# Linear attention and two gated FFNs on one core: q and x transposed in 32x32 blocks on VectorE, with loads and stores in 128-byte runs

## The chip, the cores and the metric

One core of a Trainium2 chip runs the whole kernel. The metric is the device time of one execution in microseconds (us). The kernel before took 1865.18 us, the median of three runs (1863.83 to 1867.42). Engines go by these names: PE is TensorE (PEld its weight loads), DVE is VectorE, ACT is ScalarE, POOL is GpSimd, SP is SyncE, which here only issues DMAs.

## The reference

8 batches, 8 heads, 576 positions, 64 values a head; all in float32.

```python
kv = np.einsum('bhsd,bhse->bhde', k, v)
out = np.einsum('bhsd,bhde->bhse', q, kv)
rms = np.sqrt(np.mean(out * out, axis=-1, keepdims=True) + 1e-06)
attn_out = out / rms * g_norm                      # g_norm: 64 values, the same for every head
x = attn_out.transpose(0, 2, 1, 3).reshape(4608, 512)
# first FFN (512 -> 1536 -> 512)
x = (1 / (1 + exp(-(x @ w_gate))) * (x @ w_val)) @ w_out
# second FFN, own weights
g = x @ w_gate2
x = (g * (1 / (1 + exp(-g))) * (x @ w_val2)) @ w_out2
```

## The kernel before

**The FFNs.** The 4608 tokens are cut into 9 blocks of 512, and each FFN's 1536 hidden values into 12 slices of 128. Four phases follow each other: slices 0 to 5 of the first FFN over all blocks, slices 6 to 11 of it, and the same for the second. Float32 products are made from a high and a low part, in three passes. Only the first phase shares its time with the attention and touches x in its first layout. In it `gv_plain` (L524) makes gate and value of one slice in 24 matmuls, `out_parts` (L645) multiplies the slice before by w_out in 12. The first block (block 0) is worked on while the weights of the six slices arrive: each weight tile is loaded raw (`raw`, L308 and L311), and VectorE, ScalarE and GpSimd turn it into its two parts (`o1` to `o7`, `hi`, `lo`; `u` and `s` are their buffers). From block 1 on these weights lie ready in SBUF.

**The attention.** It works on 36 tiles of 128 tokens, four to a block. Nine tiles make a pair of batches: four of the first batch, one mixed tile (i = 4) of the last 64 positions of both, four of the second batch. A tile goes through these stages, each one called for a later tile than the one before it (lags 0, 1, 3, 3, 4, 5 tiles):

- `tok_q`: the tile's q is copied out of the batch's q buffer `qm` into `qs` (ScalarE, L130; for batch 0 VectorE, L128). The mixed tile reads `qr`, loaded on its own.
- `tok_a`: four PE transposes of 128x128 into `qTp` (L165), then a ScalarE copy to `qT` (L167).
- `tok_b`: PE multiplies qT by the block-diagonal kv (L181, for the mixed tile L179), ScalarE squares the result.
- `tok_r`: VectorE sums the squares (L188), GpSimd makes the reciprocal root `y`.
- `tok_n`: VectorE multiplies by y into `xn` (L208).
- `tok_c`: four PE transposes into `xTp` (L214), ScalarE multiplies by g while it copies out to `xT` (L216; in this layout the 64 values of g lie along the partitions, in `gcol`), and one DMA stores the tile to `xd` in DRAM (L222), from where the FFN loads it as `xl` (L471).

The first four tiles (block 0) run in a prologue written out by hand (the string `PROLOGUE`); the others by `attention_steps`. The q of a batch lies in the positions p*4 + r of its partition p, so one load brings 1 KB a packet (`load_main`, L100), and the batch's 128-token tile r is every fourth position. Output rows are written in the same pattern.

**What sets the order.** The steps of the attention, the preparation of x and the weights stand in queues (`att`, `xq`, `wq`, `pq`) with due times, and `tick()` between matmuls takes from each what is due. `AHEAD = (16, 20, 24, 28, 32)` says of tiles in which block they are due: tiles before 16 in block 0, before 20 in block 1, and so on. ScalarE and GpSimd run what they are given in program order from the start; VectorE too from block 4 of the first phase on. PE, SP and, until there, VectorE get their order from a scheduler that works with a cost model. SP issues all DMAs in one stream, each when its buffer is free. The tiles named above share nine buffers of one tag (`ta`, `TA = 9`); the q and the k of a batch use two large buffers in turn (`st0`, `st1`); raw weights have three buffers.

Of the kernel before, what the change touches and what calls it, by code (L numbers as in the profile page):

```python
# [10 lines left out]
F32 = mybir.dt.float32  # L11
# [3 lines left out]
ALU = mybir.AluOpType  # L15
# [9 lines left out]
def attention_two_ffn(ctx: ExitStack, tc: tile.TileContext, q, k, v, g_norm, weights, out):  # L25
# [8 lines left out]
    nc = tc.nc  # L34
    B, H, S, D = q.shape
    DM = H * D
    DFF = weights[0][0].shape[1] // 2
    NT = B * S
    P = 128
    NB = 512  # L40
    NBLK = NT // NB
    TPB = NB // P
    KD = DM // P
    NP = H // 2
    R = 4
    SM = R * P
# [6 lines left out]
    dr = ctx.enter_context(tc.tile_pool(name="dr", bufs=1, space=DRAM))  # L53
# [6 lines left out]
    at = at_ctx.enter_context(tc.tile_pool(name="at", bufs=1, side="right"))  # L60
# [15 lines left out]
    mask = at.tile([P, P], F32, name="mask")  # L76
    gcol = at.tile([P, 1], F32, name="gcol")
    mhalf = at.tile([P, H], F32, name="mhalf")
    make_identity(nc, ident)
    nc.vector.memset(mask, 0.0)  # L80
    for e in range(2):
# [2 lines left out]


    MANUAL = (0, 4)
    TA = 9
    kvt, qt, kvps, kvbd, qT, xn, xd = {}, {}, {}, {}, {}, {}, {}
    for j in range(NBLK):
        xd[0, j] = dr.tile([P, KD, NB], F32, name=f"xd{j}")  # L90
        xd[1, j] = dr.tile([P, KD, NB], F32, name=f"yd{j}")

    def load_main(b, src, nm, halves=1):

        rows = src[b, :, :SM, :].rearrange("h (p r) d -> p h r d", r=R)
        slot = "v" if nm == "v" else f"st{b % 2 if b > 1 else 'kq'.index(nm)}"
        t = kvt[b, nm] = at.tile([P, H, R, D], F32, tag=slot, name=f"{nm}m")
        for z in range(halves):
            hs = slice(z * H // halves, (z + 1) * H // halves)
            nc.sync.dma_start(out=t[:, hs], in_=rows[:, hs])  # L100
# [9 lines left out]
        load_main(b, v, "v", 2 if b == 0 else 1)  # L110

    def load_q(b):
        load_main(b, q, "q", 2 if b == 0 else 1)

    def load_qr(bp):
        t = at.tile([P, H, D], F32, tag="qr", name="qr")
# [4 lines left out]
    def run_of(b, nm, r, hs=slice(0, H)):  # L121

        if (b, nm, r) not in kvt:
            tag, n = ("ta", TA) if b == 0 else (nm + "s", 2)
            kvt[b, nm, r] = at.tile([P, H, D], F32, tag=tag, bufs=n, name=f"{nm}s")
        t, src = kvt[b, nm, r][:, hs], kvt[b, nm][:, hs, r, :]
        if b == 0:
            nc.vector.tensor_copy(out=t, in_=src)  # L128
        else:
            nc.scalar.activation(t, src, AF.Copy)  # L130

    def bank_for(early, name):

        if early:
            return ps_o.tile([P, NP, P], F32, tag="o", name=name)
        return ps_g.tile([P, NP, P], F32, tag="g", name=name)
# [13 lines left out]

    def tok_q(tau):
        bp, i = divmod(tau, TP)
        if i != R:
            run_of(2 * bp + (i > R), "q", i if i < R else i - R - 1)

    def tok_a(tau):
        bp, i = divmod(tau, TP)
        ps = ps_g.tile([P, NP, P], F32, tag="g", name="qTp")
        for hp in range(NP):
            hs = slice(2 * hp, 2 * hp + 2)  # L160
            if i == R:
                src = qt[bp][:, hs, :]
            else:
                src = kvt[2 * bp + (i > R), "q", i if i < R else i - R - 1][:, hs, :]
            nc.tensor.transpose(ps[:, hp, :], src, ident)  # L165
        qT[tau] = at.tile([P, NP, P], F32, tag="ta", bufs=TA, name="qT")
        nc.scalar.activation(qT[tau], ps, AF.Copy)  # L167
# [3 lines left out]
    def tok_b(tau):  # L171
# [10 lines left out]
        ost[tau] = ps.rearrange("p a (b d) -> p (a b) d", d=D)  # L182
        sqt[tau] = at.tile([P, H, D], F32, tag="ta", bufs=TA, name="sq")
        nc.scalar.activation(sqt[tau], ost[tau], AF.Square)
# [20 lines left out]
    def tok_n(tau):  # L205
        y = sqt.pop(tau)
        xn[tau] = at.tile([P, H, D], F32, tag="ta", bufs=TA, name="xn")
        nc.vector.tensor_tensor(out=xn[tau], in0=ost.pop(tau), in1=y.unsqueeze(2).to_broadcast([P, H, D]), op=ALU.mult)  # L208

    def tok_c(tau):  # L210
        t = xn.pop(tau).rearrange("p (a b) d -> p a (b d)", b=2)
        ps = bank_for(tau < TPB, "xTp")
        for hp in range(NP):
            nc.tensor.transpose(ps[:, hp, :], t[:, hp, :], ident)  # L214
        x = at.tile([P, NP, P], F32, tag="ta", bufs=TA, name="xT")
        nc.scalar.activation(x, ps, AF.Identity, scale=gcol)  # L216
        j, c = divmod(tau, TPB)
        cs = slice(c * P, (c + 1) * P)
        if j == 0:
            xh, xlo = x_tiles(0, 0)  # L220
            split(xh[:, :, cs], xlo[:, :, cs], x)
        nc.sync.dma_start(out=xd[0, j][:, :, cs], in_=x)  # L222
# [57 lines left out]
    def split(hi, lo, src):  # L280
        nc.scalar.activation(hi, src, AF.Copy)  # L281
        sub(lo, src, hi.bitcast(F32))
# [170 lines left out]
    def x_tiles(ph, j):  # L453
        if (ph, j) not in xt:
            if PH[ph][3]:
                s = "RL"[((ph - 1) * NBLK + j) % 2]
                xt[ph, j] = [late[s].tile([P, 5 - i // 2, 2, HB], F32R, tag=f"x{i}", name=f"x{i}") for i in range(3)]
            else:
                xt[ph, j] = [x0p.tile([P, KD, NB], F32R, tag="x", name=f"x{b}") for b in range(2)]
        return xt[ph, j]  # L460
# [217 lines left out]
    def evac(ph, j, i):  # L678
        f = PH[ph][0]
        ps = ops.pop((ph, j, i))  # L680
        if starts(ph):
            t = wk.tile([P, NB], F32, tag="ye", bufs=4, name="ye")
            nc.scalar.activation(t, ps, AF.Copy)
        else:
            if (ph, j, i) not in part:
                load_part(ph, j, i)
            t = part.pop((ph, j, i))
            add(t, t, ps)
        if not ends(ph):
            if (ph, j) not in pd:  # L690
                pd[ph, j] = dr.tile([P, 4, NB], F32, name=f"pd{ph}_{j}")
            nc.sync.dma_start(out=pd[ph, j][:, i, :], in_=t)
        elif f == 0:
            nc.sync.dma_start(out=xd[1, j][:, i, :], in_=t)
        else:
            bp, n = divmod(j * TPB + i, TP)
            if n == R:
                for e in range(2):
                    r0 = (2 * bp + e) * S + SM
                    nc.sync.dma_start(out=out[r0:r0 + SR, :], in_=t[e * SR:(e + 1) * SR])  # L700
            else:
                r0 = (2 * bp + (n > R)) * S
                r = n if n < R else n - R - 1
                nc.sync.dma_start(out=out[r0:r0 + SM, :].rearrange("(p r) e -> p r e", r=R)[:, r, :], in_=t)

# [73 lines left out]
    for t, z in steps:  # L781
        j = next((j for j, a in enumerate(AHEAD) if t < a), len(AHEAD))
# [3 lines left out]
    wq.run(2)  # L786
    for e in range(2):
        nc.sync.dma_start(out=gcol[e * D:(e + 1) * D], in_=g_norm.unsqueeze(1))
    for z in range(2):
        for r in range(R):  # L790
            run_of(0, "k", r, slice(z * H // 2, (z + 1) * H // 2))
# [106 lines left out]
```

## Time and profile before

| | before |
|---|---|
| median of three runs | 1865.18 us |
| profiled execution | 1871.27 us, span 1869.5 us |
| granted PE clock, mean | 0.993 |
| busy: PE, PEld | 1833.5 us (98%), 1650.1 us (88%) |
| busy: DVE, ACT, POOL | 1152.0 (62%), 686.6 (37%), 597.7 us (32%) |
| DMA queue | 179312 packets, 253.80 MB, 41.6% of 16 engines |

Busy shares are means over stages with different limits, so the rows further down are cut by stretch of time. In a row of busy time by stretch stand the start and end in us from the span's start, the length, and then the busy us (with the count of instructions) of PE, PEld, DVE, ACT and POOL; an engine without work in a row that is filtered by a tile is left out; the last three numbers are the granted clock of TensorE, the mean busy share of the 16 DMA engines, and GB/s. In a short stretch the share can come out a little over 1. In the chain of waits a DMA's length runs from its issue to its landing. The PE rows of a timeline give busy time of pipelined matmuls, whose modelled ends overlap; the starts are the sounder number. In the groups by line, the tile written stands left of the arrow and those read right of it, then partitions x elements and the type.

### The profile page before, as it was taken

Reading aid. Unit: us, or ns where it says so; the run is one execution under the profiler, and the core shown is the slowest. Engines: PE = TensorE matmul, PEld = TensorE weight load, DVE = VectorE, ACT = ScalarE, POOL = GpSimd, SP = SyncE. Lnnn points to the kernel's source line nnn. Section 1 sums busy time; section 2 is a strip of 40 time slices with the busy share of each in tenths; the row PEclk is TensorE's granted clock in tenths of the full one; section 3 lists DMA queues with packets and bytes.
Section 4 is the critical chain, followed back from the end, with each engine's and each line's share of the span. In section 5 each row is a group of like instructions: output and inputs, shape, how many; then the busy total and the mean of one; then the engine's idle time right before and its main releaser. Section 6 shows DMA issues by size and latency. Waiting matters only on the chain.

```text
span 1869.5 us, 29756 instructions
## 1 busy us (share of the span) xinstructions
PE 1833.5 (98%) x11620; PEld 1650.1 (88%) x11620; DVE 1152.0 (62%) x1946; ACT 686.6 (37%) x1318; POOL 597.7 (32%) x600
## 2 busy tenths in 40 slices
PE   5899999999999999999999999999999999999999
PEld 5688888888888899999999999999999999999998
DVE  4784444444334576676666777777775566666664
ACT  3564444443323333333333343334343323232321
POOL 1574233220111433424424334334332222222221
PEclk8899999999999999999999999999999999999999
DMA  7896554336333724424429423233228222222212
GB/s 225 237 276 186 166 155 141 113 119 236 124 107 99 279 91 153 130 91 143 134 96 368 167 97 107 88 111 107 79 97 327 90 69 68 69 68 69 68 52 68
DMA packets 179453, 255.70 MB, mean 137 GB/s; under 512 B 23920, under 2 KB 123760, under 8 KB 177008
## 3 DMA queue, kind: packets, MB, share of 16 engines
q1 hardware_dynamic: 179312, 253.80, 41.6%
q8 instruction: 91, 1.49, 0.3%
q14 instruction: 50, 0.41, 0.1%
HBM read 164.10 MB, written 89.65 MB: 136 GB/s over the span
## 4 chain that ended last, share of the span: by engine, by line
PE 94%; DVE 2%; DMA 2%; POOL 1%; issue 1%; ACT 1%; SPq 0%; DVEq 0%; ACTq 0%
PE gv L586 43%; PE o L659 24%; PE gv L524 15%; PE o L645 8%; PE kvps L145 2%; PE ops L181 1%; DMA vm<-in_v_dram 1%; POOL y L191 1%; PE xTp L214 1%; DMA raw<-in_moe_w_gate_dram 1%; PE qTp L165 1%; DVE a L188 0%; PE ops L179 0%; DVE u L275 0%; POOL a L189 0%
## 5 line engine op out<-in xcount | busy, mean ns | idle before, releaser
L586 PEld LDWEIGHTS gv<-x,wgv 128*128 128x128 f32 x6804 | 821.3, 190 | 8.3 <-PE gv L586 0.6
L586 PE MATMUL gv<-x,wgv 128*128 128x256 f32 x6804 | 823.6, 282 | 0.4 <-DMA wgv<-wd 0.4
L524 PE MATMUL gv<-x,wgv 128*128 128x512 f32 x1296 | 318.9, 395 | 1.3 <-ACT qT L167 1.3
L659 PE MATMUL o<-wo,h 128*128 128x512 f32 x1296 | 311.3, 395 | 0.0
L659 PEld LDWEIGHTS o<-wo,h 128*128 128x128 f32 x1296 | 239.6, 188 | 53.8
L524 PEld LDWEIGHTS gv<-x,wgv 128*128 128x128 f32 x1296 | 238.8, 188 | 50.5 <-POOL u L200 1.7
L574 POOL TENSOR_TENSOR h<-v,h 128x512 fp32r<-128x512 f32 x81 | 112.3, 1386 | 482.3 <-ACT h L570 482.3
L275 DVE TENSOR_TENSOR u<-u,gv 128x512 f32<-128x512 f32 x162 | 110.8, 684 | 217.5 <-PE gv L586 206.7
L496 POOL TENSOR_TENSOR x<-xl,x 128x512 fp32r<-128x512 f32 x108 | 146.0, 1361 | 147.4 <-ACT x L493 131.4
L645 PE MATMUL o<-h,wo 128*128 128x512 f32 x648 | 169.1, 401 | 5.2 <-ACT h L281 5.2
L574 POOL TENSOR_TENSOR h<-w,h 128x512 fp32r<-128x512 f32 x81 | 105.2, 1299 | 207.6 <-ACT h L570 207.6
L659 PE MATMUL o<-h,wo 128*128 128x512 f32 x648 | 156.3, 396 | 2.4 <-POOL h L574 1.7
L645 PEld LDWEIGHTS o<-h,wo 128*128 128x128 f32 x648 | 119.1, 189 | 31.2 <-issue 6.0
L659 PEld LDWEIGHTS o<-h,wo 128*128 128x128 f32 x648 | 120.0, 188 | 29.6 <-POOL h L574 2.3
L557 ACT ACTIVATE w<-v 128x256 f32<-128x256 f32 x81 | 33.9, 418 | 303.3 <-DVE v L275 303.3
L570 ACT ACTIVATE h<-w 128x512 fp32r<-128x512 f32 x81 | 51.2, 633 | 192.2 <-PE o L659 95.3
L493 ACT ACTIVATE x<-xl 128x512 fp32r<-128x512 f32 x189 | 115.1, 623 | 12.0 <-DVE xl L272 9.6
L534 DVE TENSOR_TENSOR sg<-sg,gv 128x512 f32<-128x512 f32 x54 | 37.1, 686 | 106.9 <-PE gv L524 106.9
L557 ACT ACTIVATE v<-g 128x256 f32<-128x256 f32 x81 | 33.9, 418 | 152.5 <-DVE g L275 152.5
L570 ACT ACTIVATE h<-v 128x512 fp32r<-128x512 f32 x81 | 51.2, 632 | 104.9 <-DVE v L563 104.9
L496 DVE TENSOR_TENSOR x<-xl,x 128x512 fp32r<-128x512 f32 x81 | 70.8, 874 | 22.5 <-ACT x L493 22.4
L275 DVE TENSOR_TENSOR g<-u,gv 128x512 f32<-128x512 f32 x81 | 55.6, 686 | 41.3 <-PE gv L586 40.1
(88 smaller groups left out, 1910.1 us busy)
## 6 DMA issues: line engine op xcount, KB each, us to landing
wgv<-wd SPq DMA_DIRECT2D x18, 1792.0 KB, 9.7
pd<-ye SPq DMA_DIRECT2D x72, 256.0 KB, 3.0
pl<-pd SPq DMA_DIRECT2D x72, 256.0 KB, 4.2
xl<-yd SPq DMA_DIRECT2D x72, 256.0 KB, 2.9
xl<-xd SPq DMA_DIRECT2D x68, 256.0 KB, 3.1
wd<-raw SPq DMA_DIRECT2D x54, 256.0 KB, 2.8
raw<-in_moe_w_gate_dram SPq DMA_DIRECT2D x24, 512.0 KB, 4.5
raw<-in_moe_w_val_dram SPq DMA_DIRECT2D x24, 512.0 KB, 4.4
```

Of the source, the lines that this page charges most:

```text
L145: nc.tensor.matmul(kvps[b][:, hp, :], lt, rt, start=(r == hp == 0), stop=(r == R and hp == NP - 1))
L275: nc.vector.tensor_tensor(out=out, in0=a, in1=b, op=ALU.add)
L493: return lambda: nc.scalar.activation(X(o), st[i, n], AF.Copy)
L496: return lambda: eng.tensor_tensor(out=X(o + 7), in0=st[i, n], in1=X(o).bitcast(F32), op=ALU.subtract)
L524: nc.tensor.matmul(ps, w[:, e, a, kk, :], x[b][:, kk, :], start=(n == 0), stop=(n == 3 * KD - 1))
L534: nc.vector.tensor_tensor(out=sg, in0=sg, in1=bank[1], op=ALU.mult)
L557: nc.scalar.activation(o, t[:, 0], AF.Sigmoid)
L570: nc.scalar.activation(t[:, 0], v, AF.Copy)
L574: nc.gpsimd.tensor_tensor(out=t[:, 1], in0=v, in1=t[:, 0].bitcast(F32), op=ALU.subtract)
L586: nc.tensor.matmul(ps[:, e], w[:, l, kk], xs[r // 5][:, r % 5, kk], start=(fresh and e == n == kk == 0), stop=(not more and e == 1 and n = ...
L645: nc.tensor.matmul(ps, l, r, start=(fresh and t == 0), stop=(last and t == 2))
L659: nc.tensor.matmul(ps, l, r, start=(fresh and e == t == 0), stop=(last and e == 1 and t == 2))
```

## The change

For batches 2 to 7 (`QB = 2`) q is loaded by 16 DMAs a batch, each into 32 partitions, in runs of 32 values (128 bytes), so that in the buffer `qb` each block of 32 positions by 32 values stands by itself. `tok_q` then makes qT with one VectorE transpose of 32x32 blocks, and the copy to `qs`, the four PE transposes and the copy out of `qTp` are gone for these batches, except for the mixed tiles, which read `qr` as before. The tiles of these batches are now runs of 128 positions and no longer every fourth, so their output rows are contiguous too.

For tiles from 12 on (`XT = 12`) GpSimd multiplies `xn` by g (`grow`, g broadcast over the partitions by one new DMA), VectorE transposes 32x32 blocks into `xz`, and four DMAs store it to the same DRAM tile in runs of 128 bytes. The four PE transposes and ScalarE's copy of these tiles are gone. `TA` goes from 9 to 11.

```diff
-    TA = 9
+    TA = 11
+    SQ = 32
+    QB, XT = 2, 3 * TPB
+    grow = at.tile([P, D], F32, name="grow")
...
-        xd[0, j] = dr.tile([P, KD, NB], F32, name=f"xd{j}")
+        t = dr.tile([DM, NB], F32, name=f"xd{j}")
+        xd[0, j] = t.rearrange("(k p) t -> p k t", p=P)
+        xr[j] = t.rearrange("(j r) t -> r j t", r=SQ)
...
     def load_q(b):
-        load_main(b, q, "q", 2 if b == 0 else 1)
+        if b < QB:
+            load_main(b, q, "q", 2 if b == 0 else 1)
+            return
+        t = kvt[b, "q"] = at.tile([P, NP, SM // SQ, SQ], F32, tag=f"st{b % 2}", name="qb")
+        src = q[b, :, :SM, :].rearrange("(a e) (j c) (x r) -> a e x c j r", e=2, c=SQ, r=SQ)
+        for a in range(NP):
+            for i in range(4):
+                nc.sync.dma_start(out=t[i * SQ:(i + 1) * SQ, a], in_=src[a, i // 2, i % 2])
...
-            tag, n = ("ta", TA) if b == 0 else (nm + "s", 2)
+            tag, n = ("ta", TA) if b == 0 or nm == "q" else (nm + "s", 2)
...
     def tok_q(tau):
         bp, i = divmod(tau, TP)
-        if i != R:
-            run_of(2 * bp + (i > R), "q", i if i < R else i - R - 1)
+        b = 2 * bp + (i > R)
+        if b >= QB and i != R:
+            n = P // SQ
+            src = kvt[b, "q"][:, :, (i if i < R else i - R - 1) * n:][:, :, :n]
+            qT[tau] = at.tile([P, NP, P], F32, tag="ta", bufs=TA, name="qT")
+            nc.vector.transpose(qT[tau].rearrange("p a (j c) -> p a j c", c=SQ), src)
+        elif i != R:
+            run_of(b, "q", i if i < R else i - R - 1)
 
     def tok_a(tau):
         bp, i = divmod(tau, TP)
+        if tau in qT:
+            return
...
+        if tau >= XT:
+            nc.gpsimd.tensor_tensor(out=xn[tau], in0=xn[tau], in1=grow.unsqueeze(1).to_broadcast([P, H, D]), op=ALU.mult)
 
     def tok_c(tau):
+        if tau >= XT:
+            t = xn.pop(tau).rearrange("p h d -> p (h d)")
+            z = at.tile([P, DM // SQ, SQ], F32, tag="ta", bufs=TA, name="xz")
+            nc.vector.transpose(z.rearrange("p j c -> p (j c)"), t)
+            j, c = divmod(tau, TPB)
+            for i in range(P // SQ):
+                t0 = c * P + i * SQ
+                nc.sync.dma_start(out=xr[j][:, :, t0:t0 + SQ], in_=z[i * SQ:(i + 1) * SQ])
+            return
...
-                nc.sync.dma_start(out=out[r0:r0 + SM, :].rearrange("(p r) e -> p r e", r=R)[:, r, :], in_=t)
+                rows = out[r0:r0 + SM, :]
+                rows = rows.rearrange("(p r) e -> p r e", r=R)[:, r, :] if 2 * bp < QB else rows[r * P:(r + 1) * P, :]
+                nc.sync.dma_start(out=rows, in_=t)
...
+    nc.sync.dma_start(out=grow, in_=g_norm.unsqueeze(0).to_broadcast([P, D]))
```

How the order of instructions moves is read off at four places. The first is SP's queue in block 0, where the loads of batch 3's k and v and a w_gate tile stand behind the q of batch 2 (`qm` before, `qb` after; `km`, `vm` and the remainders `kr`, `vr` are k and v). Before:

```order
L308 DMA raw<-in_moe_w_out_dram 128x1024
L100 DMA qm<-in_q_dram 128x8x256
L100 DMA km<-in_k_dram 128x8x256
L104 DMA kr<-in_k_dram 64x8x64
L104 DMA vr<-in_v_dram 64x8x64
L100 DMA vm<-in_v_dram 128x8x256
L311 DMA raw<-in_moe_w_gate_dram 128x4x256
```

After:

```order
L340 DMA raw<-in_moe_w_out_dram 128x1024
L126 DMA qb<-in_q_dram 32x16x32 x16
L106 DMA km<-in_k_dram 128x8x256
L110 DMA kr<-in_k_dram 64x8x64
L110 DMA vr<-in_v_dram 64x8x64
L106 DMA vm<-in_v_dram 128x8x256
L343 DMA raw<-in_moe_w_gate_dram 128x4x256
```

One issue has become sixteen, ahead of the same loads.

The second is SP's queue where the q of batch 3 is loaded, still in block 0, between a w_gate and later weights (`xl` is a load of x for the next block, `xT` a stored tile of x). Before:

```order
L311 DMA raw<-in_moe_w_gate_dram 128x4x256
L100 DMA qm<-in_q_dram 128x8x256
L100 DMA vm<-in_v_dram 128x8x256
L222 DMA xd_97<-xT 512x1x128
L100 DMA km<-in_k_dram 128x8x256
L222 DMA xd_97<-xT 512x1x128
L104 DMA kr<-in_k_dram 64x8x64
L104 DMA vr<-in_v_dram 64x8x64
L471 DMA xl<-xd_97 128x512 x2
L311 DMA raw<-in_moe_w_val_dram 128x4x256
```

After:

```order
L343 DMA raw<-in_moe_w_gate_dram 128x4x256
L126 DMA qb<-in_q_dram 32x16x32 x4
L254 DMA xd_98<-xT 128x4x128 x2
L126 DMA qb<-in_q_dram 32x16x32 x2
L503 DMA xl<-xd_98 128x512
L126 DMA qb<-in_q_dram 32x16x32 x10
L106 DMA km<-in_k_dram 128x8x256
L110 DMA kr<-in_k_dram 64x8x64
L110 DMA vr<-in_v_dram 64x8x64
L106 DMA vm<-in_v_dram 128x8x256
L503 DMA xl<-xd_98 128x512
```

The sixteen loads no longer stand in one piece: two stores of x and a load of x stand between their parts, and k and v of batch 4 come behind them.

The third is PE in block 0, between the gate and value matmuls of slice 3 (`wgv_3`) and those of slice 4. Before:

```order
L524 MATMUL gv<-x_1108,wgv_3_913 128x512
L645 MATMUL o<-h,wo_2_790 128x512 x3
L165 MATMUL qTp<-ident,qs 128x128 x4
L645 MATMUL o<-h,wo_2_790 128x512 x6
L181 MATMUL ops<-kvbd,qT 128x128 x4
L645 MATMUL o<-h,wo_2_790 128x512 x3
L524 MATMUL gv<-x_1108,wgv_4_1123 128x512
```

After:

```order
L556 MATMUL gv<-x_1105,wgv_3_909 128x512
L677 MATMUL o<-h,wo_2_793 128x512 x9
L202 MATMUL ops<-kvbd,qT 128x128 x4
L677 MATMUL o<-h,wo_2_793 128x512 x3
L556 MATMUL gv<-x_1105,wgv_4_1120 128x512
```

The group of four transposes of q is gone; the matmuls around it keep their order.

The fourth is VectorE in block 0, among the operations that prepare weights (`u`, `s`, `raw`). Before:

```order
L275 TENSOR_TENSOR u<-u,s 128x512
L208 TENSOR_TENSOR xn<-ops,y 128x512
L188 TENSOR_REDUCE a<-sq 128x8
L318 TENSOR_SCALAR u<-u 128x512
L322 TENSOR_SCALAR u<-u 128x512
L326 SCALAR_TENSOR_TENSOR u<-raw,u 128x512
L330 TENSOR_SCALAR s<-u 128x512
L534 TENSOR_TENSOR sg<-sg,gv 128x512
```

After:

```order
L307 TENSOR_TENSOR u<-u,s 128x512
L171 STREAM_TRANSPOSE qT<-qb 128x512
L229 TENSOR_TENSOR xn<-ops,y 128x512
L209 TENSOR_REDUCE a<-sq 128x8
L350 TENSOR_SCALAR u<-u 128x512
L354 TENSOR_SCALAR u<-u 128x512
L358 SCALAR_TENSOR_TENSOR u<-raw,u 128x512
L171 STREAM_TRANSPOSE qT<-qb 128x512
L362 TENSOR_SCALAR s<-u 128x512
```

Two transposes of q into `qT` now stand in this run, which VectorE goes through in this order.

## Rows read from the trace of the kernel before

**Rows 1.** Busy time by stretch: engines' us and instructions, clock, DMA share, GB/s.

```profile
47.00:157.00 110.00, 99.86 (x612) 84.55 (x612) 81.85 (x141) 67.38 (x122) 68.93 (x100) 0.95 0.90 256
...
157.00:442.00 285.00, 285.00 (x1439) 236.78 (x1438) 133.29 (x222) 119.03 (x211) 83.28 (x138) 1.00 0.46 142
...
442.00:598.00 156.00, 156.00 (x684) 127.82 (x683) 65.18 (x103) 48.34 (x87) 16.99 (x16) 1.00 0.38 130
```

**Rows 2.** Chain of waits, 44 to 160 us: start us, length us, what.

```profile
71.67 12.48 DMA raw<-in_moe_w_gate_dram
```

**Rows 3.** Waits, 60 to 142 us: us in total, times, longest.

```profile
ACT u L315 <- DMA raw<-in_moe_w_gate_dram: 5.7, 1, 5.7
...
ACT qs L130 <- DMA qm<-in_q_dram: 4.1, 1, 4.1
```

**Rows 4.** Busy time by stretch, as rows 1, in the first block.

```profile
70.00:80.00 10.00, 8.68 (x53) 7.18 (x52) 8.73 (x16) 5.99 (x11) 8.99 (x13) 1.00 1.17 225
...
90.00:142.00 52.00, 50.69 (x322) 42.90 (x321) 42.63 (x73) 35.45 (x64) 37.36 (x56) 0.99 0.87 256
```

**Rows 5.** Timeline of PE, 200 to 262 us: start us, us, instruction, count.

```profile
234.58 0.85 PE L645 MATMUL o<-h,wo 128*128 128x512 f32 x3
...
235.27 0.60 PE L165 MATMUL qTp<-ident,qs 128*128 128x128 f32 x4
...
235.62 1.65 PE L645 MATMUL o<-h,wo 128*128 128x512 f32 x6
...
237.11 1.05 PE L181 MATMUL ops<-kvbd,qT 128*128 128x128 f32 x8
...
247.42 1.09 PE L524 MATMUL gv<-x,wgv 128*128 128x512 f32 x4
...
248.35 0.60 PE L165 MATMUL qTp<-ident,qs 128*128 128x128 f32 x4
...
248.70 2.10 PE L524 MATMUL gv<-x,wgv 128*128 128x512 f32 x8
...
250.64 1.05 PE L181 MATMUL ops<-kvbd,qT 128*128 128x128 f32 x8
```

**Rows 6.** Chain of waits, 0 to 700 us.

```profile
464.47 5.45 PE gv L524 x24
...
469.92 2.79 PE o L645 x12
```

**Rows 7.** 142 to 460 us, instructions with xTp, with qTp, with qr.

```profile
142.00:460.00 318.00, 12.56 (x84) 10.35 (x84) 14.45 (x21) 1.00 0.50 159
...
142.00:460.00 318.00, 10.17 (x68) 8.33 (x67) 10.09 (x17) 1.00 0.50 159
...
142.00:460.00 318.00, 1.20 (x8) 1.00 (x8) 1.00 0.50 159
```

**Rows 8.** Groups by line and shape: count, busy us, mean ns, idle before.

```profile
L496 POOL TENSOR_TENSOR x<-xl,x 128x512 fp32r<-128x512 f32 x108 | 146.0, 1361 | 147.4 <-ACT x L493 131.4 <-DVE u L322 15.6
...
L208 DVE TENSOR_TENSOR xn<-ops,y 128x512 f32<-128x512 f32 x36 | 24.7, 686 | 5.6 <-POOL y L202 4.8 <-PE gv L524 0.7
...
L128 DVE COPY qs<-qm 128x512 f32<-128x512 f32 x4 | 1.5, 422 | 7.8 <-DMA qm<-in_q_dram 7.8
```

**Rows 9.** DMA queue, 185 to 186, 324 to 326, 95 to 97 us: packets, MB, share.

```profile
q1 hardware_dynamic: 651, 0.16, 71.3%
...
q1 hardware_dynamic: 527, 0.26, 45.5%
...
q1 hardware_dynamic: 723, 0.74, 106.2%
```

**Rows 10.** Timeline of SP, 60 to 103 us: issue's start us, us, DMA.

```profile
63.09 0.37 SPq L100 DMA_DIRECT2D qm<-in_q_dram  x1
...
71.67 5.70 SPq L311 DMA_DIRECT2D raw<-in_moe_w_gate_dram  x1
...
101.13 0.65 SPq L104 DMA_DIRECT2D kr<-in_k_dram  x1
```

More of the change, by code (lines that the diff above doesn't have):

```diff
@@ L86, in attention_two_ffn @@
     MANUAL = (0, 4)
-    TA = 9
+    TA = 11
+    SQ = 32
+    QB, XT = 2, 3 * TPB
     kvt, qt, kvps, kvbd, qT, xn, xd = {}, {}, {}, {}, {}, {}, {}
+    xr = {}
     for j in range(NBLK):
-        xd[0, j] = dr.tile([P, KD, NB], F32, name=f"xd{j}")
+        t = dr.tile([DM, NB], F32, name=f"xd{j}")
+        xd[0, j] = t.rearrange("(k p) t -> p k t", p=P)
+        xr[j] = t.rearrange("(j r) t -> r j t", r=SQ)
         xd[1, j] = dr.tile([P, KD, NB], F32, name=f"yd{j}")
```

## The prediction

> **What bounds the kernel now.** I read the page first, then busy time by stretch, the chain of waits, the waits of one stretch, the timelines of PE and SP, and the DMA queue in short windows. The profiled execution took 1871.3 us, 1869.5 of them its span; the median of the runs shown is 1865.2, so the sum is made on 1871.3 and its difference carried to 1865.2.
>
> Busy time by stretch splits the part that the change touches [rows 1]. From 157 to 442 us PE is busy for all of 285.00 us, with the attention's small matmuls among the FFN's; from 442 to 598 it is as full with the FFN alone. From 47 to 157 us, while the first block of 512 tokens runs, PE is busy 99.86 of 110 us, the DMA engines 0.90 of the time, and VectorE 81.85 us. After 598 us the change touches nothing but the addresses of output rows that are 2 KB long before and after. So there are two regimes: behind about 142 us, PE work taken out is time taken out; ahead of it weights, DMA and VectorE set the pace together.
>
> The first regime's bottleneck shows in the chain: 12.48 us of it are one DMA, the w_gate weights issued at 71.67 us [rows 2]. ScalarE, which runs in the order written, stood 5.7 us for it, and had stood 4.1 us for the q of batch 2 just before [rows 3]. In the ten microseconds from 70 the DMA engines' busy shares add up to 1.17, which is a full queue, and from 90 to 142 us VectorE is busy 42.63 of 52 us beside a PE at 50.69 [rows 4].
>
> **What the change removes.** Per tile of 128 tokens, four PE transposes of q (24 tiles, batches 2 to 7) and four of x (tiles 12 to 35): 48 groups of four. Their price is read where PE is full, as the distance between starts less what the neighbours alone take [rows 5, 6]. From 247.42 to 250.64 us stand 12 gv matmuls and one group: 3.22 us, less 12 × 5.45/24 = 2.73, leaves 0.49. From 234.58 to 237.11 stand 9 o matmuls and one: 2.53, less 9 × 2.79/12 = 2.09, leaves 0.44. I take 0.47, not the 4 × 0.27 us that the busy column would suggest. Behind 142 us stand 84 xTp matmuls, 68 qTp, and of the latter 8 read qr, which stays [rows 7]: 84 + 60 = 144, or 36 groups. **36 × 0.47 = 16.9 us off**, all where PE waits for nobody. With them go 24 copies of q, 24 copies out of qTp and 24 out of xTp on ScalarE; it is busy 119 of the 285 us behind 157 [rows 1], so they count nothing there.
>
> The other 12 groups (48 less 36), 5.6 us of PE, lie ahead of 142 us. There VectorE takes over 12 transposes. No row shows one. Of the same 128 × 512 elements the copy takes 422 ns, the multiplication that makes xn 686 ns, and GpSimd's subtraction, the slowest, 1361 ns [rows 8]; I take 0.69 as nearest, since it also moves one element of 4 bytes in and out, and keep 0.42 and 1.36 as ends. 12 × 0.69 = 8.3 us on top of 42.63 is 50.9 of 52 us: VectorE just fills, and PE's 5.6 us are not collected. **I count 0 here**; with 0.42 a share of the 5.6 comes back, with 1.36 the stretch ends 42.63 + 16.3 - 52 = 7 us later. The Trainium skill ("VectorE: DVE Perf Modes", The three transpose paths) gives 311 ns for a 128 × 128 bf16 transpose on VectorE; four such would be an estimated 1.24 us, with which the stretch would end 5.5 us later and the kernel take 1857 us instead of 1852. No row here decides between that and 0.69.
>
> Behind 142 us the 36 transposes are 25 us of VectorE beside 133 of 285 [rows 1]: hidden, and their results are wanted three stages later. GpSimd's multiplication by g is 24 × 1.36 = 33 us [rows 8], beside 83 of 285 us; it stands between xn and the store of x, which is made one to two blocks ahead of the block that loads it (AHEAD), so it is hidden too. If GpSimd came late, the transposes queued behind it on VectorE would hold sg and h, and then PE; it has 200 us free, so I count nothing.
>
> **What the change adds in DMA.** A batch of q was one load of 1024 packets of 1 KB; it is now 16 loads of 512 packets of 128 B, 8192 in all. Three windows that hold nearly one size each give the price of a packet as share × 16 engines × length / count [rows 9]: 0.713 × 16 × 1000/651 = 17.5 ns (256 B), 0.455 × 16 × 2000/527 = 27.6 (512 B), 1.062 × 16 × 2000/723 = 47.0 (1 KB). The line through them gives about 13 ns at 128 B. The load goes from 1024 × 47/16 = 3.0 us of all engines to 8192 × 13/16 = 6.7 us. On SP it goes from one issue of 0.37 us to 16; a load of 512 packets took 0.65 us to issue [rows 10], so some 10.4 us.
>
> The first of these loads stands right ahead of k and v of batch 3 and the weights of 71.67 us, in the full queue. SP stood 5.70 us in that issue alone before [rows 10], because the queue took no more; that hides most of the longer issue, and what is left is the engines' own time, 6.7 - 3.0. **3.7 us on the chain.** Ends: below, 0, if ScalarE, which no longer waits 4.1 us for that load, makes it good; above, 10.0, if SP's issue is what ends last. VectorE now stands for the load in ScalarE's place, with sg, h and the weights' operations behind it; it idles 4 us for those weights anyway.
>
> Batches 3 and 4 load between 90 and 142 us, at a DMA share of 0.87 [rows 4]: 2 × 3.7 us into 52 × 0.13 = 6.8 us of free time. I count 0. Stores of x go from 512 packets of 512 B (0.9 us a tile) to 4 × 512 of 128 B (2048 × 13/16 = 1.7 us); behind 157 us, at a share of 0.46 [rows 1], these and the loads are hidden: 24 × 0.8 + 3 × 3.7 = 30 us into 285 × 0.54 = 154.
>
> **Sum:** -16.9 + 3.7 = -13.2: 1858.1 in a profiled execution, **1852** for the median.
>
> **Rivals.**
> *The first block gains as well.* The weights come no later, because ScalarE is 4.1 us earlier, and PE's 5.6 us are collected, because a share of the 72 copies that leave ScalarE leaves there. For it: PE at 50.69 of 52 us. Against it: VectorE's 42.63 before anything is added. -16.9 - 5.6 = -22.5: 1843 us. Chance 0.18.
> *The first block eats the gain.* The load of batch 2 costs SP's 10.0 us in full on the chain, and the load of batch 3, which in the new order has two waiting stores and a load of x between its parts, another 3.7: -16.9 + 13.7 = -3.2, 1862 us. For it: SP issues strictly in turn and weights stand behind. Against it: the 5.70 us that SP had to spare. Chance 0.14.
> *Slower: packets of 128 B cost twice the line.* The place is SP's queue ahead of 142 us, where three loads of q stand before weights that ScalarE waits for in order. At 26 ns a load is 8192 × 26/16 = 13.3 us, 10.3 more than before; three are 31: -16.9 + 31 = +14, 1879 us. It decides from 16.9/3 = 5.6 us a load, or 17 ns a packet. For it: the small packets measured are 256 B, in quiet windows; none is 128 B. Against it: their prices lie on one line. Chance 0.18. The Trainium skill ("DMA: Bandwidth & Descriptors", Specifications) says that under 512 B a DMA engine reads, modifies and writes; doubled, the stores of x would take 3.3 us a tile. The 256 B packets at 17.5 ns were reads, so no row here tests it.
>
> **How the numbers follow.** The forecast has 0.50 (its own range 1847 to 1858), the others 0.18, 0.14 and 0.18. About 0.2%, 3.7 us, is what a measurement can tell from no change. Faster by more: forecast, first rival and the edge of the second, 0.70; within: the rest of the second, 0.12; slower: 0.18. The range goes from 1841 (the first rival with cheap transposes) to 1870 (the second with dear ones) and leaves most of the third out.
>
> **What would show it.** Right: PE without qTp but for qr, 12 xTp groups, PE full from the second block on and the time from there to 598 us shorter by about 17 us; the w_gate weights that landed at 84.15 us landing near 88; 128 B packets at about 13 ns; VectorE's transposes near 0.69 us. Wrong: the second block starting more than 10 us later than at 157 us (a second or third rival), PE idle behind it for a transfer of x or for qT, VectorE transposes over 1.2 us, or GpSimd ahead of a PE wait.

## The result

The changed kernel took 1880.98 us, the median of four runs (1877.45 to 1881.06), against 1866.01 for the kernel before, now also a median of four: a ratio of 1.0077 (95% interval 1.0059 to 1.0094), slower, where 1852 us had been forecast. Its profiled execution took 1881.06 us, its span 1878.2.

Busy time by stretch, the changed kernel (columns as in [rows 1]):

```profile
47.00:157.00 110.00, 78.19 (x446) 65.21 (x445) 84.09 (x138) 46.36 (x82) 62.36 (x88) 0.86 0.78 191
157.00:442.00 285.00, 279.76 (x1351) 231.73 (x1351) 163.01 (x254) 94.97 (x172) 123.46 (x175) 0.98 0.60 156
442.00:598.00 156.00, 156.00 (x683) 127.81 (x682) 68.62 (x110) 47.17 (x85) 16.97 (x16) 1.00 0.42 139
```

The loss is in the first row. Where [rows 1] had 99.86 us of PE in 110, there are 78.19; the DMA engines are less busy (0.78, was 0.90), and so is every engine but VectorE. Taken over the whole row no engine is short of capacity; they wait for each other.

PE's waits, 60 to 180 us, the changed kernel (total, times, longest), and then ScalarE's from 90 to 142 us:

```profile
PE o L677 <- ACT h L313: 9.4, 2, 7.6
PE kvps L158 <- ACT ks L143: 6.8, 1, 6.8
PE o L677 <- DVE h L304: 6.7, 1, 6.7
...
PE kvps L158 <- DMA vm<-in_v_dram: 1.5, 1, 1.5
```

```profile
ACT u L347 <- DMA raw<-in_moe_w_val_dram: 13.3, 1, 13.3
```

In the first two PE waits for ScalarE, and ScalarE for a weight. In the third `h` comes late from VectorE, which had itself stood 2.4 us for the last parts of batch 4's q, in front of `h` in its order (VectorE's timeline):

```profile
152.38 0.71 DVE L171 STREAM_TRANSPOSE qT<-qb 128x512 f32<-128x512 f32 x1 [2.39 <-DMA qb<-in_q_dram]
...
155.39 0.65 DVE L304 TENSOR_TENSOR h<-sg,h 128x512 fp32r<-128x512 f32 x1
```

Why the weight is late stands in SP's timeline, 57 to 160 us (issue's start, us, DMA, count):

```profile
59.90 8.41 SPq L126 DMA_DIRECT2D qb<-in_q_dram  x16
...
72.17 3.29 SPq L343 DMA_DIRECT2D raw<-in_moe_w_gate_dram  x1
...
90.47 1.92 SPq L126 DMA_DIRECT2D qb<-in_q_dram  x4
95.77 2.23 SPq L254 DMA_DIRECT2D xd<-xT  x2
98.06 1.08 SPq L126 DMA_DIRECT2D qb<-in_q_dram  x2
100.08 0.35 SPq L503 DMA_DIRECT2D xl<-xd  x1
100.47 5.22 SPq L126 DMA_DIRECT2D qb<-in_q_dram  x10
...
113.41 0.43 SPq L343 DMA_DIRECT2D raw<-in_moe_w_val_dram  x1
...
134.77 1.64 SPq L126 DMA_DIRECT2D qb<-in_q_dram  x3
140.74 3.34 SPq L241 DMA_DIRECT2D xd<-xz  x4
144.12 5.83 SPq L126 DMA_DIRECT2D qb<-in_q_dram  x11
...
151.95 1.37 SPq L106 DMA_DIRECT2D vm<-in_v_dram  x1
```

The q of batch 2 goes out in one piece, 8.4 us of SP for what was one issue [rows 10]. That of batch 3 takes SP from 90.5 to 105.7 us, since two stores and a load of x stand between its parts and wait for their own sources; that of batch 4 from 130.0 to 150.0, behind stores of `xz`, which VectorE, busy 19.83 of those 20 us, makes late. Everything asked for later stands behind. In the chain of waits the late pieces appear as their landings (start, length):

```profile
72.17 9.82 DMA raw<-in_moe_w_gate_dram
...
113.41 7.00 DMA raw<-in_moe_w_val_dram
...
151.95 9.31 DMA vm<-in_v_dram
```

The prices that the prediction worked with, in the groups by line of the changed kernel (as [rows 8]), and the DMA queue from 62 to 68 us, where all packets are 128-byte loads, and from 400 to 404, where all are 128-byte stores (packets, MB, share):

```profile
L231 POOL TENSOR_TENSOR xn<-xn,grow 128x512 f32<-128x512 f32 x24 | 34.0, 1415 | 7.1 <-DVE xn L229 5.4 <-PE o L677 1.8
L237 DVE STREAM_TRANSPOSE xz<-xn 128x512 f32<-128x512 f32 x24 | 16.9, 702 | 0.6 <-POOL xn L231 0.6
L171 DVE STREAM_TRANSPOSE qT<-qb 128x512 f32<-128x512 f32 x24 | 16.7, 694 | 5.2 <-DMA qb<-in_q_dram 3.3 <-DMA wd<-raw 1.9
```

```profile
q1 hardware_dynamic: 6164, 0.77, 79.6%
...
q1 hardware_dynamic: 1364, 0.17, 29.0%
```

A transpose takes 0.69 to 0.70 us; a packet 0.796 × 16 × 6000/6164 = 12.4 ns as a load, 0.290 × 16 × 4000/1364 = 13.6 as a store.

For the comparisons below the time is cut into block 0 and blocks 1 to 7 of the first phase, read at the first gv matmul of blocks 0, 1 and 8 (24 gv matmuls to a slice, six slices to a block; the last column runs from the start of block 1 to that of block 8). In the profiled execution of before block 0 began late, at 47.7 us; over all kernels here it began between 41 and 48 us, and e8, which runs the instructions of before in the same order, began it at 42.7. So e8 is the better row to set the changed kernel against. From it to the changed kernel: start 1.3 earlier, block 0 +26.3, blocks 1 to 7 -10.0, the rest of the span +1.5, around it +1.1: the 17.6 us by which 1881.06 stands over 1863.5.

| kernel | median us | ratio to before (95%) | block 0 starts | block 0 lasts | blocks 1 to 7 |
|---|---|---|---|---|---|
| before (profiled run) | 1866.01 | | 47.7 | 109.3 | 389.8 |
| e8, before with TA = 11 | 1863.29 | 0.9996 (0.9979 to 1.0014) | 42.7 | 106.6 | 389.7 |
| changed | 1880.98 | 1.0077 (1.0059 to 1.0094) | 41.4 | 132.9 | 379.8 |
| e1, x part alone | 1855.04 | 0.9950 (0.9933 to 0.9967) | 42.4 | 107.6 | 380.6 |
| e2, q part alone | 1875.83 | 1.0066 (1.0042 to 1.0089) | 41.3 | 124.6 | 383.6 |
| e3, changed, q in 1 DMA | 1854.60 | 0.9940 (0.9922 to 0.9958) | 41.2 | 114.5 | 374.2 |
| e4, changed, q in 16 DMAs of 1 KB packets | 1865.86 | 0.9995 (0.9982 to 1.0009) | 41.8 | 119.4 | 374.2 |
| e6, before, q in 16 DMAs of 1 KB packets | 1881.68 | 1.0104 (1.0080 to 1.0129) | 43.9 | 119.7 | 389.8 |
| e7, before, q in 16 DMAs of 128 B packets | 1885.32 | 1.0127 (1.0105 to 1.0149) | 43.3 | 126.0 | 389.8 |
| e9, before, 12 transposes added | 1867.79 | 1.0016 (1.0002 to 1.0030) | 46.9 | 107.2 | 389.7 |

### The profile page after: what moved, and what is told of

It reads as the page before. It is cut to its first block, busy times and chain, and to the rows that moved or that the text cites. A ratio compares the mean times of both kernels' runs of the same rounds, so it can differ in the third digit from the quotient of the medians.

```text
span 1878.2 us, 29573 instructions
## 1 busy us (share of the span) xinstructions
PE 1815.9 (97%) x11428; PEld 1632.7 (87%) x11428; DVE 1194.5 (64%) x1994; ACT 646.2 (34%) x1246; POOL 632.6 (34%) x624
## 4 chain that ended last, share of the span: by engine, by line
PE 90%; DMA 3%; DVE 2%; SPq 2%; ACT 1%; POOL 1%; issue 1%; DVEq 0%; ACTq 0%
PE gv L618 42%; PE o L691 24%; PE gv L556 14%; PE o L677 7%; PE kvps L158 2%; DMA vm<-in_v_dram 1%; PE ops L202 1%; SPq L126 1%; DMA raw<-in_moe_w_gate_dram 1%; DMA wd<-raw 0%; POOL y L212 0%; DMA raw<-in_moe_w_val_dram 0%; DVE u L307 0%; SPq L110 0%; DVE a L209 0%
## 5 line engine op out<-in xcount | busy, mean ns | idle before, releaser
L528 POOL TENSOR_TENSOR x<-xl,x 128x512 fp32r<-128x512 f32 x108 | 146.0, 1361 | 148.9 <-ACT x L525 132.9
L566 DVE TENSOR_TENSOR sg<-sg,gv 128x512 f32<-128x512 f32 x54 | 37.1, 686 | 104.8 <-PE gv L556 104.8
L589 ACT ACTIVATE v<-g 128x256 f32<-128x256 f32 x81 | 33.9, 418 | 152.2 <-DVE g L307 152.2
L307 DVE TENSOR_TENSOR g<-u,gv 128x512 f32<-128x512 f32 x81 | 55.5, 686 | 41.2 <-PE gv L618 40.1
```

The source lines that it names most:

```text
L307: nc.vector.tensor_tensor(out=out, in0=a, in1=b, op=ALU.add)
L528: return lambda: eng.tensor_tensor(out=X(o + 7), in0=st[i, n], in1=X(o).bitcast(F32), op=ALU.subtract)
L566: nc.vector.tensor_tensor(out=sg, in0=sg, in1=bank[1], op=ALU.mult)
L589: nc.scalar.activation(o, t[:, 0], AF.Sigmoid)
```

## The experiments

**The two halves (e1, e2).** Edits: the number of the first batch and of the first tile.

```diff
-    QB, XT = 2, 3 * TPB
+    QB, XT = B, 3 * TPB            # e1
+    QB, XT = 2, NT // P            # e2
```

> The x part alone: QB = 8, so no q is transposed on VectorE; q loads are one DMA each again; XT = 12 and TA = 11 stay. Theory S (the sixteen issues of a load of q, 0.53 us each on SP, stand in front of k, v and weights in block 0) and theory P (their 128-byte packets fill the DMA queue in block 0): block 1 starts within 5 us of the 157 us of the kernel before, and the 21 groups of PE transposes of x behind it go: 1866 - 21 x 0.47 = 1856 us. Theory V (VectorE, with its transposes and their waits, holds up block 0): 4 or 5 of 17 transposes stay in block 0, so block 1 starts some 5 us late and the time is about 1861.

> The q part alone: XT = 36, so x is transposed on PE and stored in 512-byte runs as before. S and P: block 0 keeps nearly all of its loss (17 us), block 1 starts at 170 us or later, and 15 groups of PE transposes of q go behind it: 1866 + 15 - 7 = 1874 us, from 1870 to 1880. V: 12 of 17 transposes stay in block 0: block 1 near 169, 1871 us.

Measured: 1855.0 and 1875.8. The x part is worth its transposes: blocks 1 to 7 are 9.2 us shorter for 21 groups, 0.44 each, and block 0 is as long as in e8 within 1.0. The q part saves 6.1 us for 15 groups and loses 18.1 in block 0. Together block 0 loses 26.3, 7 more than the sum. The changed kernel's chain of waits shows a path for it: VectorE up to 140.7 us, SP's stores of `xz` and the last eleven parts of q behind them, k, and the v of batch 5 that lands at 161.3. e1's time speaks against V as the main cause; e2 does not decide, since block 1 began at 166.0 us, earlier than any theory had it (169, or 170 and later). S and P stand.

**The load of q taken apart (e3, e4).** The changed kernel, with its buffer filled in the old layout.

```diff
+        nc.sync.dma_start(out=w, in_=q[b, :, :SM, :].rearrange("h (p r) d -> p h r d", r=R))      # e3
...
+        for h in range(H):                                                                        # e4
+            for i in range(2):
+                ps = slice(i * P // 2, (i + 1) * P // 2)
+                nc.sync.dma_start(out=w[ps, h], in_=rows[ps, h])
```

> As the changed kernel, but the q of a batch from 2 on comes in one DMA of 1 KB packets into the same buffer; VectorE transposes what lies there, so its values are not the reference's. S and P: block 1 starts at about 158 us and the time is 1881 - 16 = 1865, or less. V: block 1 stays near 174 us and the time near 1880.

> As the changed kernel, but the sixteen DMAs of a load of q bring 64 packets of 1 KB each in place of 512 of 128 bytes; the values are not the reference's. S: the sixteen issues stay, so block 1 stays near 172 us and the time near 1879. P: block 1 near 161 us, about 1868. V: 174 and 1880.

Measured: 1854.6 and 1865.9. With one load the change is a gain of 0.6%, all VectorE work included, so V is out as the main cause. Sixteen issues take 11.3 us back, and the step from e4 to the changed kernel another 15.1. Neither S nor P alone: e4's numbers are those expected of P, but by P alone e3 would have taken as long. The 15.1 are not the packets' alone, since the scheduler also put SP's queue in another order: the second load of q, with its stores between, lasts 11.2 us in e4 and 15.2 in the changed kernel. The issue does not pay by the packet: sixteen DMAs of 64 packets took e4's SP longer than sixteen of 512 took the changed kernel's (8.41 us):

```profile
57.04 10.09 SPq L128 DMA_DIRECT2D qb<-in_q_dram  x16
```

What arrives late is read off the landings of the loads behind each q (us from the span's start, the four kernels' block 0 beginning within 1.5 us of each other):

| landed | e8 | e3 | e4 | changed |
|---|---|---|---|---|
| w_gate, behind the q of batch 2 | 77.1 | 78.8 | 79.9 | 82.0 |
| v of batch 4, behind the q of batch 3 | 93.6 | 95.8 | 110.2 | 118.4 |
| w_val, behind the same | 104.8 | 105.5 | 113.5 | 120.4 |
| v of batch 5, behind the q of batch 4 | 132.5 | 138.0 | 148.7 | 161.3 |

Behind the three loads of q the lateness is 4.9, 24.8 and 28.8 us in the changed kernel, 2.8, 16.6 and 16.2 with 1 KB packets. The q itself is late too: its last part landed at 70.3, 108.1 and 152.2 us in the changed kernel, the one load of e8 at 65.6, 90.3 and 121.3.

**Only late batches (e5).** QB = 5, with XT = 12. The rows of the output of batch 5 are stored in the old pattern here, so they lie elsewhere than they should; the work is the same.

> As the changed kernel, but with QB = 5: only the q of batches 5 to 7, which SP loads behind block 0, comes in runs of 128 bytes and is transposed on VectorE; x as in the x part alone (XT = 12). If the loss is block 0's loads of q (S and P together), block 1 starts where it did with the x part alone (150 us), and 12 more groups of PE transposes go behind it at 0.43 us, as one block's length gave: 1855 - 5 = 1850 us. If loads of q in 128-byte runs hurt wherever they are, the time is 1855 or more.

Measured: 1857.3 (ratio 0.9963, 0.9947 to 0.9978). Block 1 began at 150.2 us, as with the x part alone, but blocks 1 to 7 took 382.4, 1.8 more than there instead of 5 less. The load of batch 6's q stood in 209.5 to 237.1 us of SP's timeline, with stores between its parts; k, v, stores of weights and a w_out stand behind it. ScalarE stood 9.6 us for the w_out and 6.0 for VectorE, and PE for ScalarE (PE's waits, 150 to 560 us):

```profile
PE kvps L158 <- ACT ks L143: 4.4, 1, 4.4
```

So a load in sixteen parts hurts behind block 0 too, in one place.

**The load alone, in the kernel before (e6, e7).** No VectorE work moves; in e7 the buffer is laid out in runs of 32 values, and ScalarE's copy puts them right.

```diff
+        for h in range(H):
+            for i in range(2):
+                ps = slice(i * P // 2, (i + 1) * P // 2)
+                nc.sync.dma_start(out=t[ps, h], in_=rows[ps, h])        # e6
+                nc.sync.dma_start(out=t[ps, :, h], in_=rows[ps, h])     # e7
```

> The kernel before with one edit: the q of batches 2 to 7 comes in sixteen DMAs of 64 packets of 1 KB each, same values, same place, nothing on VectorE. If the sixteen issues alone cost time (S): 6 to 11 us more than before, 1872 to 1877. If only small packets do (P): 1866.

> The kernel before, with the q of batches 2 to 7 in sixteen DMAs of 512 packets of 128 bytes each, as many issues and packets as in the changed kernel; the buffer is laid out in another order of 32-value runs, which ScalarE's copy to qs puts right. Nothing moves to VectorE and all PE transposes stay. S and P together: 13 to 20 us more than before, 1880 to 1886, and 8 to 13 more than with sixteen DMAs of 1 KB packets. S alone: as with these. If it was VectorE that held block 0 (V): within 4 us of before.

Measured: 1881.7 and 1885.3. The sixteen issues alone cost 17.6 us, more than expected, and small packets only 3.6 on top, less than expected; the sum, 21.2, is just over the 13 to 20 expected. SP's timeline of e6 has the same long turns:

```profile
59.82 10.07 SPq L121 DMA_DIRECT2D qm<-in_q_dram  x16
...
88.73 6.92 SPq L121 DMA_DIRECT2D qm<-in_q_dram  x11
```

In e7 the first sixteen took SP 10.79 us. What the DMA engines did during the two turns of e6 decides between them and SP (busy time by stretch):

```profile
59.82:69.89 10.07, 10.07 (x65) 8.82 (x64) 9.48 (x17) 3.31 (x6) 9.09 (x13) 1.00 0.49 144
88.73:100.25 11.52, 11.52 (x78) 10.08 (x77) 7.13 (x13) 5.78 (x11) 6.56 (x13) 1.00 0.45 132
```

They are busy 0.49 and 0.45 of the time, where [rows 4] has 0.87 for most of the block: while SP issues sixteen small DMAs, the DMA engines are half idle. So the turn is SP's, not theirs. In the changed kernel the shares are 0.80, 0.57 and 0.51 in its three turns, and VectorE is busy for all of the third:

```profile
59.90:68.31 8.41, 8.41 (x58) 7.47 (x57) 7.90 (x16) 4.98 (x10) 7.51 (x12) 1.00 0.80 162
90.47:105.69 15.22, 15.07 (x100) 13.01 (x99) 10.97 (x20) 7.53 (x13) 10.05 (x17) 1.00 0.57 115
129.95:149.95 20.00, 16.22 (x93) 13.07 (x91) 19.83 (x30) 8.51 (x15) 15.08 (x17) 1.00 0.51 98
```

The step to sixteen issues costs 11 in the changed kernel and 18 in the old one, the step to small packets 15 and 4; what else stands in the queue, and in what order, goes into both.

**More buffers (e8), VectorE alone (e9).** e8 is TA = 11; e9 has TA = 11 too and adds a transpose a tile, for batches 2 to 4, into a buffer that nobody reads.

```diff
+            z = at.tile([P, 2, R * D], F32, tag="ta", bufs=TA, name="zz")
+            nc.vector.transpose(z.rearrange("p h c -> p (h c)"), kvt[b, "q"][:, 0:2].rearrange("p h r d -> p (h r d)"))
```

> The kernel before with TA = 11 in place of 9, and the copies of q of batch 1 on drawn from the same buffers; every engine runs the same instructions in the same order. If the two buffers are what let the first slice of block 0 start 6 us earlier in all kernels that have them: first slice at about 42 us in place of 47.7, and 0 to 6 us off the time, 1860 to 1866, as far as block 0 is not held by its loads. If the new order did that: no difference, 1866.

> The kernel before (with TA = 11, which changed nothing) and 12 VectorE transposes of 128 x 512 added in block 0, one for each tile of batches 2 to 4, into a buffer that nobody reads: 8.4 us of VectorE and nothing else. V: VectorE is full there, so block 0 gets 5 to 8 us longer and the time 1869 to 1873. If VectorE has room: within 2 us of the 1864 before.

Measured: 1863.3, no difference. The early start of block 0 is not the buffers' either: with nine of them e6 and e7 began it at 43.9 and 43.3 us, with eleven e9 at 46.9. What sets it was not found. With the transposes 1867.8, 2.1 us more than before and between the two expectations; block 0 lasts 0.6 longer than in e8. VectorE absorbs most of the 8.4 us, in a buffer that nobody waits for. Where the transposes stand between q and PE they cost more: e3, with one load, has a block 0 of 114.5 us, e1 one of 107.6. VectorE is full in e3's stretch from 110 to 140 us, of which PE has 22.67, and not in e1's; first e3, then e1:

```profile
110.00:140.00 30.00, 22.67 (x137) 18.05 (x135) 29.97 (x48) 12.59 (x24) 23.89 (x31) 0.95 0.78 214
```

```profile
110.00:140.00 30.00, 28.43 (x176) 23.46 (x175) 28.71 (x47) 19.85 (x38) 24.98 (x32) 1.00 0.75 211
```

**Which of the loads (e10).** e6 with `if b not in (3, 4)` in front of the old load.

> The kernel before, with the q of batches 3 and 4 alone in sixteen DMAs of 1 KB packets; batch 2 and 5 to 7 in one. The prediction counted the loads of batches 3 and 4 at nothing. S, as the issue times of the sixteen-DMA run give it (k and v of the next batch stand behind each load): about 9 of its 17 us, 1873. If only the first load counts: 1864.

Measured: 1879.6 (1.0094, 1.0070 to 1.0118), 13.9 us over before: most of e6's 17.6, and more than either number expected. In the trace block 0 is 8.3 us longer than e8's (e6's is 13.2 longer); another 5.0 us between the two traces lie ahead of block 0, which began at 47.7 us, with no split load before it. What waits there, 100 to 146 us:

```profile
ACT u L323 <- DMA raw<-in_moe_w_val_dram: 9.4, 1, 9.4
ACT qs L138 <- DMA qm<-in_q_dram: 7.2, 2, 6.4
...
PE xTp L222 <- ACT qT L175: 4.3, 1, 4.3
...
PE ops L189 <- ACT qT L175: 3.4, 1, 3.4
```

PE's 4.3 us end behind the w_val that stood in SP's queue behind the q of batch 3, its 3.4 behind the q of batch 4 itself; in the chain of waits the parts of that q, issued one after another from 128.7 to 138.9 us, stand right ahead of them. The loads that the prediction had counted at zero are the dear ones.

**Another place in the queue (e11, e12).** In the changed kernel k and v of batch b + 2 are asked for ahead of the q of batch b + 1; e12 has QB = 6 as well.

```diff
-                    st.append((t, lambda b=b: load_q(b + 1)))
                     if b + 2 < B:
                         st.append((t, lambda b=b: load_kv(b + 2)))
+                    st.append((t, lambda b=b: load_q(b + 1)))
```

> The changed kernel with one swap: k and v of batch b + 2 are asked for ahead of the q of batch b + 1 (L280s, attention_steps), so that they no longer stand behind its sixteen issues on SP. If it is what stands behind the issues in SP's queue that ends last, block 0 gets shorter by the waits for v that PE had there, some 6 to 8 us, and the time is 1873 to 1876; if the whole queue of DMA work counts, in whatever order, 1881.

> The x part alone (XT = 12) with the q of batches 6 and 7 transposed on VectorE (QB = 6) and k and v asked for ahead of q: 8 more groups leave PE. If the swap keeps the loads of q out of the way, 1855 - 3.4 = 1851.6 us; if the sixteen issues still delay what stands behind them, as with QB = 5, 1855 to 1858.

Measured: 1888.5 (1.0131, 1.0111 to 1.0150) and 1863.3 (0.9991, 0.9978 to 1.0005). Both expectations of e11 missed: the wait only changed its name. With q later, PE's waits, 30 to 180 us, are

```profile
PE xTp L246 <- DVE xn L229: 16.6, 3, 11.8
PE o L677 <- DVE h L304: 12.7, 1, 12.7
```

for VectorE, which in the same stretch stood 23.9 us in its transposes for q. e12 missed both of its expectations too: the swap lengthened block 0 to 113.2 us, though no q of block 0 was split.

**Another engine's queue (e13, e14).** `nc.sync.dma_start` becomes `nc.scalar.dma_start`, one DMA to a step; e13 is e6 so changed, e14 the changed kernel.

> The kernel before, with the q of batches 2 to 7 in the same sixteen DMAs of 1 KB packets that cost 17 us on SP, but issued by ScalarE, between its other work, so that k, v, weights and stores on SP stand behind none of them. If the loss is SP's turn (S), most of it goes: 1864 to 1870. If sixteen DMAs cost the same wherever they are issued (the DMA engines or their queue), or ScalarE's turn is as dear as SP's: 1878 to 1884.

> The changed kernel with its loads of q issued by ScalarE in place of SP, one by one between its steps. If SP's turn is the cause, the issues' share goes (11 us, as between sixteen DMAs and one of 1 KB packets) and the packets' share may stay (15 us): 1865 to 1872; if the packets hurt only because all else stood behind them on SP, 1856 to 1862. If not: 1878 or more.

Measured: 1896.5 (1.0170, 1.0144 to 1.0195) and 1895.7 (1.0166, 1.0144 to 1.0189). ScalarE's turn is dearer than SP's. In e13's timeline of ScalarE six issues took 9.93 us, with the DMA engines busy 0.96 of the time from 99 to 110 us, and its waits name them:

```profile
99.73 9.93 ACTq L121 DMA_DIRECT2D qm<-in_q_dram  x6
```

```profile
ACT wgv L368 <- DMA qm<-in_q_dram: 9.6, 2, 5.5
...
ACT u L325 <- DMA qm<-in_q_dram: 6.9, 2, 4.3
```

The Trainium skill ("Trainium Kernel Development and Optimization", Key Constraints) says that DMAs issued from several engines run on the same 16 engines, and that issuing from more than one saves only issue time. Here even that was not saved, since ScalarE had work in order behind it. So these two do not tell SP's turn from the DMA engines; they show that with ScalarE issuing, ScalarE's own work pays.

**A version that could beat both (e15).** QB = 6, old order of the loads.

> The x part with QB = 6 and the loads in the old order: only the q of batches 6 and 7 on VectorE. If the swap was what cost 5 us in the run before: block 1 at 150 us and 1852 to 1855, against the 1855 of the x part alone; if loads of q in sixteen parts hurt here too, 1856 or more.

Measured: 1858.5 (0.9971, 0.9958 to 0.9984): faster than before, not than the x part alone. Block 1 began at 150.0 us, as with the x part alone, so the swap had been at fault in e12 (160.1); blocks 1 to 7 took 383.2, with the same 4.4 us wait as in e5. That is what was expected if loads in sixteen parts hurt here too. Of the versions with every value in its place e1 is the best, 0.5% under before.

## Why the prediction was wrong

Forecast were +3.7 us in block 0 and -16.9 behind it; measured against e8, +26.3 and -10.0. Of the 26.3, 18.4 go with the way q is loaded (the changed kernel less e3), 7.9 remain with one load (e3 less e8).

*Gain behind block 0, -16.9 us.* Right in mechanism and nearly in size: -15.6 in e3 (0.43 us a group and not 0.47). In the changed kernel only -10.0 is left: PE stands 3.7 us up to 290 us for a `ks` that ScalarE makes late, after waiting 7.9 us for a w_out that stood, with stores of weights, behind the load of batch 6 in SP's queue (232 to 260 us) and 6.0 for VectorE, and from 290 to 300 us the granted clock is 0.83.

*Prices.* VectorE's transpose was taken at 0.69 us and takes 0.69 to 0.70. The 1.24 estimated from the Trainium skill's figure ("VectorE: DVE Perf Modes", The three transpose paths) does not hold for this shape and type. A 128-byte packet was taken at 13 ns and takes 12.4 to 13.6, stores included. The slower rival, whose time of 1879 came close, rested on 26 ns and is wrong in its mechanism: its time was luck. The rule of the Trainium skill beside it ("DMA: Bandwidth & Descriptors", Specifications), read as a doubling, is not borne out for loads or stores here. GpSimd's multiplication took 1.42 us for the 1.36 taken, and PE waited for none.

*First load, 3.7 us on the chain.* Near in size, but not for the reason given. w_gate landed 4.9 us later than in e8; the prediction had SP's longer issue hidden and only the DMA engines' longer packets left, yet e4, with the old packets, already lands it 2.8 later, and e3, with one load, 1.7. SP did not hide its issue: it reached the w_gate at 72.17 us, 6.6 later than in e8.

*The step that failed: "Batches 3 and 4 load between 90 and 142 us, at a DMA share of 0.87 [rows 4]: 2 × 3.7 us into 52 × 0.13 = 6.8 us of free time. I count 0."* Their loads made v of batches 4 and 5 land 24.8 and 28.8 us late, and w_val 15.6; e10 took 13.9 us more with these two loads alone split, at 1 KB packets. Even on its own terms 7.4 us do not fit into 6.8. Two things beyond that were wrong in it. It used the mean share of the DMA engines as room that anything can use, but SP serves one queue in turn, and what stands behind the sixteen issues starts later however free the engines are: in e6 they were busy 0.49 and 0.45 of SP's turns. And it charged SP only for the first load: with two stores and a load of x between the parts, the second turn lasted 15.2 us, with stores of `xz` the third 20.0, of which the issues of q themselves are 8.2 and 8.4. The rival in which the first block eats the gain had this mechanism, priced at 10.0 for the first load and 3.7 for the second (13.7; the way q is loaded cost 18.4 in block 0).

*VectorE just fills, count 0.* Half right: it is full (29.97 of 30 us in e3) and PE's groups were not collected, but beyond that block 0 got 6.9 us longer than in e1. By e9 it is not the busy time alone. In e3 PE's longest wait there, 4.8 us up to 138.7, is for an `h` whose `sg` VectorE reached at 137.2, right behind a transpose of q; that the order of VectorE's queue is the cause was not tested.

*Stores of x hidden.* Right with the x part alone (block 0 +1.0 over e8), not where SP was late: block 0 of the changed kernel is 8.2 us longer than that of the q part alone. The x part brings VectorE's transposes as well as the stores, and no run separates the two.

What stays open: how much of the step to 128-byte packets (15 us in the new kernel, 4 in the old) is the DMA engines' own time and how much the other order of SP's queue, and what the sixteen parts would cost in a queue on which nothing else waits; this was not tried. The two loads that hurt most are also those that the scheduler mixed with waiting stores, and these two were not separated.

## What to carry to other kernels

A transfer cut into sixteen is paid for in its queue: count its issues (here 0.5 to 0.7 us each) for every load and not only the first, add the waits of what the scheduler puts between the parts, and follow what stands behind. A mean free share of an engine or of the DMA queue over a stretch is not room for work that is served in turn. When a change has two halves, price and time them apart: here one was worth 0.5%, and the other lost more in block 0 (18.1 us) than the two gained behind it (9.2 and 6.1).

## What was not expected of the hardware

The issue time of a DMA does not follow its packets: sixteen of 64 packets of 1 KB took SP 10.1 us, sixteen of 512 packets of 128 bytes 8.4 into 32 partitions each and 10.8 into 64. Stores of 128 bytes cost the DMA engines 13.6 ns a packet, hardly more than loads. A 32x32-block transpose of 128 x 512 float32 on VectorE costs 0.70 us, what a multiplication of that shape does. And waits are paid twice on PE: where the changed kernel's PE had stood still for 7.6 and 6.8 us (up to 83.4 and 123.3 us), the ten microseconds in which the wait ends have a granted clock of 0.53, near the lower of the two levels (1.2 GHz), and of 0.66, between it and the upper (2.4):

```profile
80.00:90.00 10.00, 6.60 (x28) 6.03 (x29) 7.09 (x12) 5.30 (x10) 2.46 (x6) 0.53 0.62 204
...
120.00:130.00 10.00, 6.69 (x41) 5.51 (x42) 8.61 (x15) 7.19 (x14) 5.92 (x7) 0.66 0.74 225
```
